# Sparse attention with a folded network: start-up loads in another order, value means copied by GpSimd, fewer engines with a written order

## The chip, the cores and the metric

The kernel runs on one core of one Trainium2 chip. The metric is device time in microseconds (us), from the start to the end of one execution; lower is better. The engines named below are TensorE (PE in the profile, with PEld for its weight loads), VectorE (DVE), ScalarE (ACT), GpSimd (POOL) and SyncE (SP), which here only issues transfers. One execution was also run under the hardware profiler; "the profile" and "the trace" are what it recorded.

## The reference

Attention over 4 batches, 8 heads, 768 positions, head size 64. Each position attends to the 31 positions around it and to 24 block summaries (the maximum of the keys of a block of 32, the mean of its values). The result is the input of a small network of four weight matrices, with no non-linearity but one product.

```python
k_sum = k.reshape(B, H, nb, block, D).max(axis=3)
v_sum = v.reshape(B, H, nb, block, D).mean(axis=3)
scores_l = scale * np.matmul(q, k.transpose(0, 1, 3, 2))     # kept where |i - j| < 16
scores_s = scale * np.einsum('bhsd,bhnd->bhsn', q, k_sum) + np.log(block)
a = softmax(concatenate([scores_l_m, scores_s], axis=-1))
x = np.matmul(a, concatenate([v, v_sum], axis=2))            # then 3072 tokens x 512
return ((x @ w1) * (x @ w2)) @ w3 @ w_out
```

## The kernel before

**Pairs and units.** Attention is done in 32 pairs: a pair is two heads (128 rows of head size) over half a batch (384 positions). Four pairs make a unit, whose four x tiles feed the network for 384 tokens. For one pair TensorE does the scores (`sc`, 6 matmuls, recorded in 12 halves), the transposes of the exponentials (`tp`) and the outputs (`po`); VectorE adds the mask and takes the minimum of the negated scores (L277), ScalarE does the exponentials (L291), and the results are split in a high and a low part for the float32r products (`keep_x`). The transposes of the first 8 pairs multiply by diagonals of the reciprocal sums; the later ones have the exponentials normalized by GpSimd (L300).

**Weights.** w3 and w_out are multiplied once (`fold_weights`: `wp[i]`, eight of 24 matmuls each), so that a unit costs the two products with w1 and w2 (`gate`: 16 accumulations of 12 matmuls, `mm<-x,w`) and one with `wp` (`project`). The weights come as 64-bit floats in 40 **pieces** of 128x512 (p0 to p39: eight of w_out, sixteen of w3, sixteen of w1 and w2). `piece` converts one: ScalarE L133, VectorE L139 and L140 (the 32-bit value), ScalarE L150 (its high part), VectorE L87 (its low part). Two pieces fill one tile `w`, and a matmul of `fold_weights` needs the piece that holds its columns. A piece's raw words lie in one of ten buffers (tag "ring"), which the rows of v for the means, batch 0's keys and later the `h` tiles share.

**The start.** A loop over steps t handles one piece a step, with the loads, the eight first pairs and the folding woven in: `FIRST` gives the step at which each of the first eight pairs begins, `LOADS` the extra transfers that follow a piece's, `WORK` the vector work of a step, `RATE` how much folding a step may emit. TensorE's stream takes from `stream` as many products as a step is due. Inside `manual_schedule(engines=...)` the engines named keep the order in which the code emits; the others are ordered by a scheduler from its own estimates. In this loop that is all five engines; in the loop behind it (pairs 8 to 31) only TensorE.

**The means of v.** For batch 0 the value means are a product: six matmuls (L219) of a constant matrix `mean_sb`, which is loaded, with rows of v. They come out at partitions 0 to 23, are copied to `vs0` (L537), and SyncE's transfers (L241, `load_sums`) carry them to the two partition ranges of each pair's value tile `v`, from 96 and from 32. Later batches take their means from `vB` on VectorE (L206, L207).

Of the kernel before, what the change touches and what calls it, by code (L numbers as in the profile page):

```python
# [11 lines left out]
F32 = mybir.dt.float32  # L12
# [14 lines left out]
PIECE = 512  # L27
AHEAD = 6

FIRST = (4, 8, 12, 16, 29, 34, 40, 43)  # L30
RING = 10


# [12 lines left out]
    return out  # L46


def mean_constants(n):

    rows = np.arange(n).reshape(-1, P).T
    return np.where(rows[:, :, None] // BLOCK == np.arange(n // BLOCK), 1.0 / BLOCK, 0.0).astype(np.float32)


@with_exitstack
def attention_moe(ctx, tc, qG, kW, kT, vP, vW, vB, mask, mean, w1, w2, w3T, wo, out):
    nc = tc.nc
    B, NPAIR, _, S = kT.shape
    NB = S // BLOCK
# [21 lines left out]
    halves = const.tile([P, 64], F32, name="halves")  # L81
    nc.gpsimd.tensor_tensor(halves, ident[:, :64], ident[:, 64:], ALU.add)
    mask_sb = const.tile([P, 3, COLS], F32, name="mask_sb")
    wp = [const.tile([P, 2, DO], F32R, name=f"wp{i}") for i in range(NF)]

    def low(eng, dst, src, hi):
# [21 lines left out]
        for at in range(0, n, PIECE):  # L108
            todo.append((src, shape, keep, at, min(n, at + PIECE)))

    begun = [0]
# [104 lines left out]
    def mean_products(tiles):  # L216
        po = ps.tile([P, 512], F32, name="means", tag="sc", bufs=4)
        for i in range(S // P):
            nc.tensor.matmul(  # L219
                po[:NB, :DM],  # L220
                lhsT=mean_sb[:, i],
                rhs=tiles[i // 2][:, i % 2],
                start=i == 0,
                stop=i == S // P - 1,
            )
        return po
# [118 lines left out]

    def keep_x(po, x):
        t = sb.tile([P, 2, U], F32R, name="x", bufs=7)
        full = sb.tile([P, U], F32, name="full")
        nc.scalar.copy(t[:, 0], po[:, :U])
        nc.vector.tensor_copy(full, po[:, :U])  # L350
        low(nc.vector, t[:, 1], full, t[:, 0])
        x.append(t)


# [2 lines left out]
    def gate(f, x, hs):  # L357
        acc = []
        for w in range(2):
            k = f * P // FQ  # L360
            while done[0] < NFOLD + PT * (2 * k + w + 1) or len(x) < NC:
                yield 0
            t = w12[w][k]
            fs = slice(f * P % FQ, f * P % FQ + P)
            a = ps.tile([P, 512], F32, name="mm", bufs=2)
            for c in range(NC):
                products(
                    a[:, :U],
                    [(t[:, 0, c, fs], x[c][:, 0]), (t[:, 1, c, fs], x[c][:, 0]), (t[:, 0, c, fs], x[c][:, 1])],
                    c == 0,  # L370
                    c == NC - 1,
                )
                yield 3 * U
            acc.append(a)
            if w == 0:
                g = sb.tile([P, U], F32, name="g")
                nc.scalar.copy(g, a[:, :U])  # L377
        nc.vector.tensor_tensor(g, acc[1][:, :U], g, ALU.mult)  # L378
        h = sb.tile([P, 2, U], F32R, name="h", tag="ring", bufs=RING)
        nc.vector.tensor_copy(h[:, 0], g)  # L380
# [110 lines left out]
    def first_pair(s):  # L491

        if s:
            prepare(s)
        u, sm, mx, sc = begin(s)
        yield
        fetch(s + 2)
# [5 lines left out]
        if s > 1:  # L503
# [18 lines left out]
    def later(work):  # L522
        delayed.append([2, work])

    kraws, vraws = {}, []

    def keys(p):
        kraws[p] = load_keys(0, p)

# [3 lines left out]
    def means():  # L533
        po = mean_products(vraws)
        vraws.clear()
        vs[0] = sb.tile([NB, DM], F32, name="vs0", tag="vs0", bufs=1)
        nc.scalar.copy(vs[0], po[:NB, :DM])  # L537

    mean_sb = aligned([P, S // P, NB], name="mean_sb", tag="sm", bufs=2)
    LOADS = {  # L540
        1: [lambda: keys(0), lambda: fetch(0)],
        3: [lambda: nc.sync.dma_start(mask_sb, mask)],
        4: [lambda: keys(1), lambda: fetch(1)],
        6: [lambda: nc.sync.dma_start(mean_sb, mean), lambda: rows(0)],
        7: [lambda: rows(1)],
        8: [lambda: rows(2)],
        10: [lambda: keys(2)],
        11: [lambda: fetch_values(0)],
        14: [lambda: fetch_values(1)],
        15: [lambda: keys(3)],  # L550
    }
    WORK = {
        2: [lambda: summaries(0, 0, kraws.pop(0)), lambda: fill(0)],
        6: [lambda: summaries(0, 1, kraws.pop(1))],
        8: [means],
        10: [lambda: fetch_sums(0), lambda: summaries(0, 2, kraws.pop(2))],
        12: [lambda: fetch_sums(1)],
        14: [lambda: summaries(0, 3, kraws.pop(3))],
    }
    RATE = 4600  # L560

    engines = mybir.EngineType
    with tc.manual_schedule(engines={engines.SP, engines.PE, engines.Activation, engines.DVE, engines.Pool}):
# [129 lines left out]
```

## Time and profile before

| what | value |
|---|---|
| median of 3 runs | 583.47 us (582.5 to 583.69) |
| the profiled execution's own time | 583.32 us |
| its span in the trace | 581.5 us |
| PE busy | 548.9 us, 94% of the span, 3948 matmuls |
| PEld busy | 486.1 us, 84% |
| DVE busy | 319.1 us, 55% |
| ACT busy | 220.2 us, 38% |
| POOL busy | 70.4 us, 12% |

Busy time is a share of the whole span, and the stages differ: the start is told from rows by time. A row of the timeline gives start, length, engine, line, what is written from what, and in brackets the idle time ahead of it with what ended it. A row of the chain of waits gives start, length and what the end of the program hung on at that time. A row of the groups gives busy time and the mean length of one in ns, then the idle time just ahead of the group's instructions and what ended it. Instructions of one engine overlap at their ends, so that in a dense stretch the distance from start to start is what one costs.

### The profile page before, as it was taken

What the parts mean: (1) busy time and instruction counts of PE and PEld (TensorE: products, weight loads), DVE (VectorE), ACT (ScalarE), POOL (GpSimd) and SP (SyncE); (2) the same over time, 40 slices, a digit from 0 to 9 for tenths busy, and PEclk for the clock granted to TensorE, in tenths of its full rate; (3) what the DMA queues carried; (4) which work ended last, traced back from release to release, by engine and by line L of the source; (5) the groups of instructions that cost most, each with busy time, mean ns of one, the idle gap of its engine ahead of it and who ended that gap; (6) DMA issues with size and microseconds to landing.
All of it is one profiled execution on the core that took longest, in us unless ns stands there. A gap on an engine that the chain in (4) does not pass through costs nothing.

```text
span 581.5 us, 10478 instructions
## 1 busy us (share of the span) xinstructions
PE 548.9 (94%) x3948; PEld 486.1 (84%) x3948; DVE 319.1 (55%) x872; ACT 220.2 (38%) x674; POOL 70.4 (12%) x96
## 2 busy tenths in 40 slices
PE   0768999999999999999999999999999999999997
PEld 0337787898789988998899989998999899988995
DVE  4857899797467532696246524662466246622330
ACT  4566776563533333333333233323332333331101
POOL 1000000000011211101111111111111111110000
PEclk9798999999999999999999999999999999999999
DMA  8998995523674122163221122112211222000001
GB/s 314 401 327 237 268 337 165 149 73 114 195 220 141 59 77 96 59 176 103 84 80 56 49 93 67 50 51 95 78 59 60 95 78 59 1 37 19 1 1 55
DMA packets 36290, 68.02 MB, mean 117 GB/s; under 512 B 4880, under 2 KB 19856, under 8 KB 36240
## 3 DMA queue, kind: packets, MB, share of 16 engines
q1 hardware_dynamic: 32784, 61.06, 33.1%
q10 hardware_dynamic: 3456, 6.29, 2.9%
q8 instruction: 31, 0.51, 0.4%
q14 instruction: 19, 0.16, 0.1%
HBM read 58.68 MB, written 6.29 MB: 112 GB/s over the span
## 4 chain that ended last, share of the span: by engine, by line
PE 86%; DVE 5%; DMA 4%; SPq 2%; ACT 1%; issue 1%; DVEq 0%; ACTq 0%
PE mm L91 72%; PE sc L263 5%; PE po L337 4%; PE tp L318 2%; PE tp L320 2%; DMA wraw<-in_wo_dram 1%; PE means L219 1%; DMA k<-in_kW_dram 1%; DMA v<-vs 1%; DMA raw<-in_vB_dram 1%; DVE sm L277 1%; ACT sm L291 1%; DVE ks L189 1%; DVE vs L206 1%; SPq L241 1%
## 5 line engine op out<-in xcount | busy, mean ns | idle before, releaser
L91 PE MATMUL mm<-x,w 128*128 128x384 f32 x1536 | 274.5, 336 | 2.6 <-DVE g L378 1.1
L91 PEld LDWEIGHTS mm<-x,w 128*128 128x128 f32 x1536 | 265.9, 188 | 7.1 <-DVE g L378 2.0
L91 PE MATMUL mm<-wp,h 128*128 128x512 f32 x576 | 137.2, 393 | 0.0
L91 PEld LDWEIGHTS mm<-wp,h 128*128 128x128 f32 x576 | 106.7, 188 | 22.5 <-issue 0.2
L377 ACT COPY g<-mm 128x384 f32<-128x384 f32 x64 | 30.6, 479 | 167.0 <-PE mm L91 167.0
L291 ACT ACTIVATE sm<-sm,mx 128x184 f32<-128x184 f32 x192 | 84.0, 440 | 17.6 <-DVE mx L277 17.5
L378 DVE TENSOR_TENSOR g<-mm,g 128x384 f32<-128x384 f32 x64 | 35.2, 551 | 88.9 <-PE mm L91 87.9
L326 DVE COPY pt<-tp 120x384 f32<-120x384 f32 x32 | 17.8, 556 | 87.0 <-PE tp L318 86.1
L277 DVE CUSTOM_DVE_ANT_0 sm<-sc,mask_sb 128x184 f32<-128x184 f32 x192 | 54.9, 345 | 5.9 <-PE sc L263 4.1
L296 POOL TENSOR_SCALAR mx<-mx 128x6 f32<-128x6 f32 x32 | 11.0, 345 | 387.9 <-ACT sm L291 355.5
L91 PE MATMUL mm<-w,w 128*128 128x512 f32 x192 | 49.6, 408 | 5.4 <-DVE w L87 5.3
L263 PE MATMUL sc<-k,q 64*128 64x184 f32 x384 | 39.5, 339 | 13.4 <-POOL k L252 13.4
L300 POOL TENSOR_TENSOR sm<-sm,mx 128x1104 f32<-128x1104 f32 x24 | 49.0, 2042 | 6.6 <-DVE mx L297 6.6
L91 PEld LDWEIGHTS mm<-w,w 128*128 128x128 f32 x192 | 35.8, 192 | 15.9 <-DVE w L87 6.6
L263 PEld LDWEIGHTS sc<-k,q 64*128 64x128 f32 x384 | 31.6, 196 | 15.4 <-POOL k L252 13.4
L325 ACT COPY pt<-tp 120x384 f32<-120x384 f32 x32 | 15.3, 478 | 65.3 <-PE tp L318 63.1
L380 DVE CAST h<-g 128x384 fp32r<-128x384 f32 x64 | 38.7, 605 | 2.0
L337 PEld LDWEIGHTS po<-pt,v 120*64 120x64 f32 x768 | 25.8, 140 | 14.3 <-issue 12.5
L87 DVE TENSOR_TENSOR h<-g,h 128x384 fp32r<-128x384 f32 x64 | 35.7, 558 | 2.0
L337 PE MATMUL po<-pt,v 120*64 120x64 f32 x768 | 30.3, 229 | 6.7 <-DMA v<-vs 6.1
L291 ACT ACTIVATION_READ_ACCUMULATOR sm<-sm,mx 128x1 f32 x192 | 36.2, 188 | 0.0
L397 ACT COPY wf<-mm 128x512 f32<-128x512 f32 x24 | 14.0, 581 | 53.7 <-PE mm L91 53.7
(32 smaller groups left out, 318.7 us busy)
## 6 DMA issues: line engine op xcount, KB each, us to landing
k<-in_kW_dram SPq DMA_DIRECT2D x32, 276.0 KB
wraw<-in_w3T_dram SPq DMA_DIRECT2D x16, 512.0 KB
wraw<-in_w_dram SPq DMA_DIRECT2D x16, 512.0 KB
raw<-in_kT_dram SPq DMA_DIRECT2D x16, 384.0 KB
q<-in_qG_dram SPq DMA_DIRECT2D x32, 192.0 KB
out_dram<-wf ACTq DMA_DIRECT2D x24, 256.0 KB
v<-in_vW_dram SPq DMA_DIRECT2D x32, 144.0 KB
raw<-in_vB_dram SPq DMA_DIRECT2D x12, 384.0 KB
```

The source lines that it names most:

```text
L87: eng.tensor_tensor(dst, src, hi.bitcast(F32), ALU.subtract)
L91: nc.tensor.matmul(acc, lhsT=a, rhs=b, start=first and i == 0, stop=last and i == len(terms) - 1)
L263: nc.tensor.matmul(sc[i // 2][h][:, i % 2 * COLS : (i % 2 + 1) * COLS], lhsT=q[rows, i * P : (i + 1) * P], rhs=k[rows, i], start=True, sto ...
L277: nc.vector.tensor_tensor_reduce(out=sm[:, j], in0=sc[i // 2][h][:, i % 2 * COLS : (i % 2 + 1) * COLS], in1=mask_sb[:, 0 if blk == 0 else ...
L291: nc.scalar.activation(sm[:, j], sm[:, j], AF.Exp, bias=mx[:, 0, j : j + 1], scale=-1.0, accum_out=mx[:, 1, j : j + 1])
L300: nc.gpsimd.tensor_tensor(sm, sm, mx[:, 2].unsqueeze(2).broadcast_to([P, NI, COLS]), ALU.mult)
L325: nc.scalar.copy(pt[0], tp[0][:KR, :U])
L326: nc.vector.tensor_copy(pt[1], tp[1][:KR, :U])
L337: nc.tensor.matmul(po[cols, at : at + 64], lhsT=v[:, g, i, cols], rhs=pt[g][:, (h * NBLK + i) * 64 : (h * NBLK + i + 1) * 64], start=True, ...
L377: nc.scalar.copy(g, a[:, :U])
L378: nc.vector.tensor_tensor(g, acc[1][:, :U], g, ALU.mult)
L380: nc.vector.tensor_copy(h[:, 0], g)
```

## The change

Six things change:

1. **The order of the first loads.** `LOADS` puts batch 0's keys, the mask, the rows of v and the later q, k and v tiles behind other pieces; `start_loads` issues an extra load only while the ring has room; q and k of pairs 2 and 3 and v of pairs 2 and 3 are loaded from this table. `FIRST` and `WORK` move to match.
2. **The value means of batch 0.** `mean_sb` is [128, 6, 128], set by GpSimd's memsets instead of a load, with the nonzero columns at 32 to 55 and 96 to 119. The product (now 120 rows instead of 24) so writes the means at both partition ranges, and GpSimd copies them into `v` instead of SyncE's transfers.
3. **No copy `full` in `keep_x`:** VectorE's low part reads the PSUM tile.
4. **The high part of `h` in `gate`** is cast by ScalarE instead of VectorE.
5. **Batch 1's blocks and keys** (the `coming` table) are loaded three and two pairs ahead instead of five to two.
6. **The start's `manual_schedule` names SP and PE only;** ScalarE, VectorE and GpSimd are ordered by the scheduler there too.

```diff
-FIRST = (4, 8, 12, 16, 29, 34, 40, 43)
+FIRST = (9, 13, 17, 21, 29, 33, 37, 41)
...
+    mean_sb = const.tile([P, S // P, P], F32, name="mean_sb")
+    nc.gpsimd.memset(mean_sb, 0.0)
+    for i in range(P // BLOCK):
+        for at in (CUT, CUT - 64):
+            part = mean_sb.rearrange("p t n -> p (t n)")[i * BLOCK : (i + 1) * BLOCK, at + i :: P + P // BLOCK]
+            nc.gpsimd.memset(part[:, : S // P], 1.0 / BLOCK)
...
-    def start_loads(n):
-        while todo and len(loading) < n:
+    def start_loads(at_least):
+        while todo or due_loads:
+            if len(loading) >= at_least and len(loading) + len(kraws) + len(vraws) + made[0] + 3 >= RING:
+                return
+            if due_loads:
+                due_loads.pop(0)()
+                continue
+            if len(loading) >= AHEAD:
+                return
...
-            for load_ in LOADS.pop(begun[0], ()):
-                load_()
+            due_loads.extend(LOADS.pop(begun[0], ()))
...
-                po[:NB, :DM],
-                lhsT=mean_sb[:, i],
+                po[:KR, :DM],
+                lhsT=mean_sb[:, i, :KR],
...
         for g, at in enumerate((CUT, CUT - 64)):
-            nc.sync.dma_start(v[at : at + NB, g], src.unsqueeze(1).broadcast_to([NB, NBLK, P]))
+            if b:
+                src = vs[b][p * NB : (p + 1) * NB]
+                nc.sync.dma_start(v[at : at + NB, g], src.unsqueeze(1).broadcast_to([NB, NBLK, P]))
+            else:
+                src = vs[b][at : at + NB, p * P : (p + 1) * P]
+                nc.gpsimd.tensor_copy(v[at : at + NB, g], src.unsqueeze(1).broadcast_to([NB, NBLK, P]))
...
-        full = sb.tile([P, U], F32, name="full")
         nc.scalar.copy(t[:, 0], po[:, :U])
-        nc.vector.tensor_copy(full, po[:, :U])
-        low(nc.vector, t[:, 1], full, t[:, 0])
+        low(nc.vector, t[:, 1], po[:, :U], t[:, 0])
...
-        nc.vector.tensor_copy(h[:, 0], g)
+        nc.scalar.copy(h[:, 0], g)
...
-        for at, step in zip((5, 5, 4, 4, 3, 3, 2, 2), steps):
+        for at, step in zip((3, 3, 3, 3, 2, 2, 2, 2) if b == 1 else (5, 5, 4, 4, 3, 3, 2, 2), steps):
...
-        8: [means],
-        10: [lambda: fetch_sums(0), lambda: summaries(0, 2, kraws.pop(2))],
+        12: [lambda: summaries(0, 1, kraws.pop(1)), means],
+        14: [lambda: fetch_sums(0)],
...
-    with tc.manual_schedule(engines={engines.SP, engines.PE, engines.Activation, engines.DVE, engines.Pool}):
-        start_loads(AHEAD)
+    with tc.manual_schedule(engines={engines.SP, engines.PE}):
+        start_loads(0)
```

Where it moves instructions is seen in the built programs. The first place is SyncE's queue at the very start; `wraw<-in_wo_dram` and `wraw<-in_w3T_dram` are pieces of w_out and w3, `raw` the keys for the summaries. Before:

```order
L117 DMA wraw<-in_wo_dram 128x1024 x2
L184 DMA raw<-in_kT_dram 128x768
L247 DMA q<-in_qG_dram 128x384
L248 DMA k<-in_kW_dram 128x552
L117 DMA wraw<-in_w3T_dram 128x1024 x2
L542 DMA mask_sb<-in_mask_dram 128x552
L117 DMA wraw<-in_wo_dram 128x1024
```

And SyncE's queue of the changed program from its start, up to the rows of v for the means:

```order
L128 DMA wraw<-in_wo_dram 128x1024 x2
L128 DMA wraw<-in_w3T_dram 128x1024 x2
L128 DMA wraw<-in_wo_dram 128x1024 x3
L194 DMA raw<-in_kT_dram 128x768
L261 DMA q<-in_qG_dram 128x384
L262 DMA k<-in_kW_dram 128x552
L128 DMA wraw<-in_wo_dram 128x1024 x2
L552 DMA mask_sb<-in_mask_dram 128x552
L128 DMA wraw<-in_wo_dram 128x1024
L128 DMA wraw<-in_w3T_dram 128x1024
L223 DMA rows<-in_vP_dram 128x2x512 x2
```

Seven pieces now stand ahead of pair 0's keys instead of two. Behind these rows follow a piece, the third of the three loads of `rows`, and the keys, q and k of pair 1.

The second place is TensorE's queue from its start. `mm<-w,w` is folding (24 matmuls for one `wp`), `means` the product with `mean_sb`. Before:

```order
L263 MATMUL sc<-k,q 128x184 x6
L91 MATMUL mm<-w_120,w_145 128x512 x6
L91 MATMUL mm<-w_178,w_145 128x512 x6
L219 MATMUL means<-rows,mean_sb 24x512 x6
L263 MATMUL sc<-k,q 128x184 x6
L91 MATMUL mm<-w_223,w_145 128x512 x6
L320 MATMUL tp<-diag,sm 120x64 x12
L91 MATMUL mm<-w_286,w_145 128x512 x6
L337 MATMUL po<-pt,v 64x64 x12
```

The same queue of the changed program, from its start to pair 0's transposes:

```order
L93 MATMUL mm<-w_115,w_137 128x512 x6
L93 MATMUL mm<-w_157,w_137 128x512 x6
L93 MATMUL mm<-w_183,w_137 128x512 x6
L277 MATMUL sc<-k,q 128x184 x6
L93 MATMUL mm<-w_211,w_137 128x512 x6
L229 MATMUL means<-rows,mean_sb 120x512 x6
L93 MATMUL mm<-w_115,w_257 128x512 x6
L93 MATMUL mm<-w_157,w_257 128x512 x3
L277 MATMUL sc<-k,q 128x184 x6
L93 MATMUL mm<-w_157,w_257 128x512 x3
L93 MATMUL mm<-w_183,w_257 128x512 x6
L334 MATMUL tp<-diag,sm 120x64 x12
```

The first 24 folding matmuls now all stand ahead of the means, and 24 more stand between the means and what follows; behind these rows come 18 folding matmuls and then pair 0's `po`.

The third place is where the value means reach `v`. Before, in SyncE's queue, between pieces of w3 (`v<-vs_263` are the means, `k` and `q` those of pair 3):

```order
L184 DMA raw<-in_kT_dram 128x768
L247 DMA q<-in_qG_dram 128x384
L248 DMA k<-in_kW_dram 128x552
L117 DMA wraw<-in_w3T_dram 128x1024
L241 DMA v<-vs_263 24x3x128 x2
L117 DMA wraw<-in_w3T_dram 128x1024 x2
```

In the changed program they stand in GpSimd's queue, ahead of the sums of pair 1's exponentials (`mx`):

```order
L266 COPY k<-ks 128x3x24
L310 TENSOR_SCALAR mx<-mx 128x6
L266 COPY k<-ks 128x3x24
L255 COPY v<-vs_301 24x384 x4
L310 TENSOR_SCALAR mx<-mx 128x6
L266 COPY k<-ks 128x3x24
L255 COPY v<-vs_301 24x384 x4
```

Sixteen such copies, two for each of the eight pairs of batch 0, take the place of sixteen transfers.

More of the change, by code (lines that the diff above doesn't have):

```diff
@@ L46, in mask_constants, with attention_moe @@
     return out
-def mean_constants(n):
-    rows = np.arange(n).reshape(-1, P).T
-    return np.where(rows[:, :, None] // BLOCK == np.arange(n // BLOCK), 1.0 / BLOCK, 0.0).astype(np.float32)
 @with_exitstack
-def attention_moe(ctx, tc, qG, kW, kT, vP, vW, vB, mask, mean, w1, w2, w3T, wo, out):
+def attention_moe(ctx, tc, qG, kW, kT, vP, vW, vB, mask, w1, w2, w3T, wo, out):
     nc = tc.nc
@@ L109, in weight @@
             todo.append((src, shape, keep, at, min(n, at + PIECE)))
-    begun = [0]
-    def start_loads(n):
-        while todo and len(loading) < n:
+    begun, due_loads, kraws, vraws = [0], [], {}, []
+    def start_loads(at_least):
[7 more added lines that the diff above has]
+                return
             src, shape, keep, at, to = todo.pop(0)
@@ L496, in first_pair @@
         yield
-        fetch(s + 2)
+        if s + 2 >= NPAIR:
+            fetch(s + 2)
         reduce(u, 0, sc, sm, mx)
@@ L502, in first_pair @@
         yield
-        if s > 1:
+        if s >= NPAIR:
             fetch_values(s)
@@ L523, in later @@
         delayed.append([2, work])
-    kraws, vraws = {}, []
     def keys(p):
@@ L535, in means @@
         vraws.clear()
-        vs[0] = sb.tile([NB, DM], F32, name="vs0", tag="vs0", bufs=1)
-        nc.scalar.copy(vs[0], po[:NB, :DM])
-    mean_sb = aligned([P, S // P, NB], name="mean_sb", tag="sm", bufs=2)
+        vs[0] = sb.tile([KR, DM], F32, name="vs0", tag="vs0", bufs=1)
+        nc.scalar.copy(vs[0], po[:KR, :DM])
     LOADS = {
[L541 to L550, printed above, removed]
+        6: [lambda: keys(0), lambda: fetch(0)],
+        8: [lambda: nc.sync.dma_start(mask_sb, mask)],
+        10: [lambda: rows(0), lambda: rows(1)],
+        11: [lambda: rows(2), lambda: keys(1), lambda: fetch(1)],
+        13: [lambda: fetch_values(0)],
+        14: [lambda: keys(2), lambda: fetch(2)],
+        16: [lambda: fetch_values(1)],
+        18: [lambda: keys(3), lambda: fetch(3)],
+        20: [lambda: fetch_values(2)],
+        22: [lambda: fetch_values(3)],
     }
     WORK = {
-        2: [lambda: summaries(0, 0, kraws.pop(0)), lambda: fill(0)],
-        6: [lambda: summaries(0, 1, kraws.pop(1))],
-        8: [means],
-        10: [lambda: fetch_sums(0), lambda: summaries(0, 2, kraws.pop(2))],
-        12: [lambda: fetch_sums(1)],
-        14: [lambda: summaries(0, 3, kraws.pop(3))],
+        8: [lambda: summaries(0, 0, kraws.pop(0)), lambda: fill(0)],
+        12: [lambda: summaries(0, 1, kraws.pop(1)), means],
+        14: [lambda: fetch_sums(0)],
+        16: [lambda: summaries(0, 2, kraws.pop(2)), lambda: fetch_sums(1)],
+        20: [lambda: summaries(0, 3, kraws.pop(3))],
+        21: [lambda: fetch_sums(2)],
+        23: [lambda: fetch_sums(3)],
     }
@@ L568, in attention_moe @@
         while next_piece or old or pairs or delayed or t <= FIRST[-1]:
-            start_loads(max(1, min(AHEAD, RING - 3 - made[0])))
+            start_loads(1)
             now, next_piece = next_piece, None
@@ L666 @@
     mask = mask_constants(NB, scale)
-    mean = mean_constants(S)
     def words(w, n):
@@ L680 @@
     for name, a in (
-        ("qG", qG), ("kW", kW), ("kT", kT), ("vP", vP), ("vW", vW), ("vB", vB), ("mask", mask), ("mean", mean),
+        ("qG", qG), ("kW", kW), ("kT", kT), ("vP", vP), ("vW", vW), ("vB", vB), ("mask", mask),
         ("w1", tiles(moe_w1)), ("w2", tiles(moe_w2)), ("w3T", w3T), ("wo", wo),
```

1 line of the change is left out of this document (removed).

## The prediction

> **What bounds the kernel now.** The page first: how busy is TensorE, and when is it not? The second row is its busy share in 40 slices of 14.5 us.
>
> ```profile
> span 581.5 us, 10478 instructions
> PE   0768999999999999999999999999999999999997
> ```
>
> From the fifth slice on TensorE is full; only the first four hold waits. So the time is TensorE's work plus what it waits at the start, and nothing off TensorE counts unless TensorE waits for it. The timeline of TensorE shows the waits one by one (in brackets, with what ended them):
>
> ```profile
> 13.41 2.21 PE L263 MATMUL sc<-k,q 64*128 64x184 f32 x12 [13.41 <-POOL k L252]
> ...
> 20.55 0.96 PE L91 MATMUL mm<-w,w 128*128 128x512 f32 x3 [1.36 <-DVE w L87]
> 23.88 0.80 PE L91 MATMUL mm<-w,w 128*128 128x512 f32 x1 [2.37 <-DVE w L87]
> 24.61 7.11 PE L219 MATMUL means<-rows,mean_sb 128*24 128x512 f32 x12
> ...
> 38.87 0.50 PE L91 MATMUL mm<-w,w 128*128 128x512 f32 x1 [1.56 <-DVE w L87]
> 45.51 1.55 PE L337 MATMUL po<-pt,v 120*64 120x64 f32 x24 [6.14 <-DMA v<-vs]
> ```
>
> The groups show all that TensorE waited after that: 2.6 for the gates, 0.8 for a transpose, and in the `po` group 0.6 besides the 6.1 above, 4.0 us in all.
>
> ```profile
> L91 PE MATMUL mm<-x,w 128*128 128x384 f32 x1536 | 274.5, 336 | 2.6 <-DVE g L378 1.1 <-ACT g L377 0.6 <-DVE w L87 0.6
> L320 PE MATMUL tp<-diag,sm 64*120 64x64 f32 x192 | 12.2, 269 | 0.8 <-DVE full L350 0.8
> L337 PE MATMUL po<-pt,v 120*64 120x64 f32 x768 | 30.3, 229 | 6.7 <-DMA v<-vs 6.1 <-ACT pt L325 0.6
> ```
>
> The chain of waits gives the price of each kind of work where TensorE is dense, and the slow stretch after its long wait:
>
> ```profile
> 39.69 5.68 DMA v<-vs
> ...
> 45.51 1.55 PE po L337 x24
> 47.06 1.97 PE sc L263 x12
> ...
> 60.12 1.14 PE sc L263 x12
> ...
> 63.53 1.41 PE tp L320 x24
> 64.93 4.31 PE mm L91 x18
> 69.24 0.85 PE po L337 x24
> ...
> 577.96 0.58 ACT wf L397
> ```
>
> A folding matmul costs 4.31 / 18 = 0.239 us, the scores of a pair 1.14, its transposes 1.41, its outputs 0.85. TensorE ends at 577.96; the last copy and store take 3.54 more of the span.
>
> The wait of 6.14 is the largest that can go. The means were ready long before:
>
> ```profile
> 31.76 0.57 ACT L537 COPY vs<-means 24x512 f32<-24x512 f32 x1 [4.44 <-PE means L219]
> ```
>
> They were copied by 32.3, but SyncE issued their transfer at 39.69, after the loads queued ahead of it, and it landed at 45.4. And a wait costs twice: the windows show the granted clock (the first figure behind POOL's) fall.
>
> ```profile
> 21.50:22.50 1.00, 0.01 (x1) 0.00 (x0) 1.00 (x3) 1.00 (x4) 0.02 (x1) 0.50 1.06 414
> ...
> 43.00:45.50 2.50, 0.00 (x0) 0.02 (x1) 0.00 (x0) 0.00 (x0) 0.00 (x0) 0.50 0.98 316
> ```
>
> Half the clock makes `po` 1.55 instead of 0.85 and the next `sc` 1.97 instead of 1.14: 1.5 us behind the long wait.
>
> **The change, part by part: up to the means.** TensorE's matmuls are the same in number and in columns moved. The sum goes by one milestone, the end of the means (24.61 + 7.11 = 31.72 before).
>
> Loads first. Piece 0 (512 KB, from 128x1024 words) was taken up at 4.90, piece 7, before which 6660 KB had been asked for, at 21.37:
>
> ```profile
> 4.90 0.66 ACT L133 ACTIVATE wf<-wraw 128x512 f32<-128x512 f32 x1 [2.90 <-DMA wraw<-in_wo_dram]
> ...
> 21.37 0.66 ACT L133 ACTIVATE wf<-wraw 128x512 f32<-128x512 f32 x1 [1.64 <-DMA wraw<-in_wo_dram]
> ```
>
> That is (6660 - 512) / 16.47 = 373 KB a us. In the new order the third load of rows ends at 8808 KB, so at 27.1, pair 1's k at 9660 KB, 29.4, and pair 0's v at 10972 KB, 33.0. Seven pieces in a row arrive every 1.4 us, and VectorE takes longer for each, as rows of a dense stretch show:
>
> ```profile
> 94.63 0.68 DVE L87 TENSOR_TENSOR w<-wf,w 128x512 fp32r<-128x512 f32 x1
> 95.23 0.41 DVE L139 TENSOR_SCALAR wf<-wf 128x512 uint32<-128x512 uint32 x1
> 95.68 0.69 DVE L140 SCALAR_TENSOR_TENSOR wf<-wraw,wf 128x512 uint32<-128x512 uint32 x1
> 96.29 0.69 DVE L87 TENSOR_TENSOR wp<-mm,wp 128x512 fp32r<-128x512 f32 x1
> 96.89 0.34 DVE L277 CUSTOM_DVE_ANT_0 sm<-sc,mask_sb 128x184 f32<-128x184 f32 x1
> ...
> 97.16 0.34 DVE L277 CUSTOM_DVE_ANT_0 sm<-sc,mask_sb 128x184 f32<-128x184 f32 x1
> ```
>
> From start to start a piece is 0.60 + 0.45 + 0.61 = 1.66, a store of `wp` 0.60, a reduction 0.27. So VectorE, not the loads, paces the new start. It begins with piece 0:
>
> ```profile
> 5.59 0.43 DVE L139 TENSOR_SCALAR wf<-wf 128x512 uint32<-128x512 uint32 x1 [5.59 <-ACT wf L133]
> ```
>
> Ahead of the means stand all 24 matmuls of the first fold, which need pieces 0 to 9: ten pieces 16.6, one key summary 0.95 (group row below), three reductions 0.8, and about 0.8 of waits for ScalarE's parts: 24.8, the last three matmuls 0.7, so the means start at 25.5. Their fifth matmul needs the third load of rows at 27.1, when four of 0.86 or more have run (28.9): covered by 1.8. They took 7.11 before, partly at half clock; the dense end below gives 0.43 a record, 5.1 for twelve.
>
> ```profile
> 29.41 2.31 PE L219 MATMUL means<-rows,mean_sb 128*24 128x512 f32 x5
> ```
>
> Bounds: 25.5 + 5.1 = 30.6, and 25.5 + 7.1 with 1.1 more if the scores too run at half clock, 33.7. I take **32.0**, the middle. The load of `mean_sb` goes; GpSimd's nine memsets, at some 0.24 each by its shortest copy below, lie in its idle time long before 25.5.
>
> The Trainium skill has a rule here (TensorE: Matmul & The Clock Gate, "Why this matters for your kernels"): no TensorE gaps over about 3 us, or the clock halves. The new start has no gap over 2 us after its first matmul, so by it the means would run at full clock, and the sum below would be 1.4 lower. The rows above disagree: the clock was already 0.50 at 21.5 after waits of 1.36 and less.
>
> **After the means.** Before, from 31.72 to 577.96 are 546.2 us. Off go the waits 1.56 + 6.14 + 4.0 and the slow 1.5: 533.0 of dense work. The order of TensorE has 12 more folding matmuls done ahead of the means, 2.9 less: **530.1**. What does TensorE wait now?
>
> - The sums of v: ScalarE copies the means at 32.0 + 0.6, GpSimd copies them to `v`. `po` stands behind 36 folding matmuls, the scores of pair 1 and a transpose: 8.6 + 1.1 + 1.4 = 11.2 after the means, 43.2; pair 0's v is there at 33.0. The price of a copy of 24x384 isn't in the trace; nearest are a 128x72 copy, 0.24, and the two-input 128x1104, 2.03, which by elements would be 0.71:
>
> ```profile
> 22.48 0.24 POOL L252 COPY k<-ks 128x72 f32<-128x72 f32 x1 [9.13 <-DVE ks L189]
> ...
> 305.31 2.03 POOL L300 TENSOR_TENSOR sm<-sm,mx 128x1104 f32<-128x1104 f32 x1 [0.31 <-DVE mx L297]
> 305.69 1.86 DVE L380 CAST h<-g 128x384 fp32r<-128x384 f32 x1
> ...
> 308.82 0.36 DVE L380 CAST h<-g 128x384 fp32r<-128x384 f32 x1
> ```
>
>   Four copies are at most 2.8 us: the 6.14 and its 1.5 go, with some 7 us of cover.
> - VectorE's order has piece 11's low part behind two reductions of pair 1's scores: TensorE waits about **0.5**.
> - VectorE is full from there to the last fold. By the order of the built program it does, from pair 1's first reduction to the last store of `wp`, 21 pieces, 24 reductions, 7 stores, 8 evacuations and 2 key summaries:
>
> ```profile
> L326 DVE COPY pt<-tp 120x384 f32<-120x384 f32 x32 | 17.8, 556 | 87.0 <-PE tp L318 86.1 <-PE tp L320 0.5
> L189 DVE TENSOR_REDUCE ks<-raw 128x24 f32<-128x768 f32 x16 | 15.0, 946 | 1.8 <-DMA raw<-in_kT_dram 1.8
> ```
>
>   34.9 + 6.5 + 4.2 + 4.5 + 1.9 = 52.0, from 3.1 after the means (nine folding matmuls 2.2, then the scores' first tile 0.9): done 55.1 after the means; the last fold's own end puts its store at 55.9. TensorE needs that store, to reuse the accumulator, when 168 folding matmuls, four pairs' `sc`, `tp`, `po` and one accumulation of 2.3 are done: 40.2 + 13.6 + 0.5 + 2.3 = 56.6. Slack 0.7. The rows above also show GpSimd stopping VectorE: the cast took 1.86 beside GpSimd's 2.03, and 0.36 alone. Ten of the copies fall in this stretch, between 0 and 7 us of VectorE. I take 2 (they get in between some operations, beside others that read PSUM nothing): **1.4** of wait, bounds 0 and 6.4.
> - Of the later 4.0, between none and all stay: **2.1**, the middle, since `full` (32 of 0.56) and the casts (64) leave VectorE but the gates still wait for g; the casts on ScalarE, some 0.5 us each by its copies, come between TensorE's needs (with that cover gone, the slower rival below). GpSimd's and VectorE's new order from the scheduler I cost at nothing beyond these: the weights' low parts lie several us ahead of TensorE.
>
> Sum: 32.0 + 530.1 + 0.5 + 1.4 + 2.1 = 566.1, the tail 3.54 makes a span of 569.6, and 1.8 outside the span (583.32 - 581.5) **571.5 us**, against 583.32 of the same execution, which is 0.15 below the median of the runs. The 11.8 gained are the 6.14, 1.5 and 1.56, the 2.9 of folding done sooner, less 0.3.
>
> **The rivals.**
>
> *VectorE becomes the bound at the first gates.* For: it was busy 17.45 of 18 us there before, and the slack is 0.7.
>
> ```profile
> 80.00:98.00 18.00, 18.00 (x106) 14.69 (x106) 17.45 (x36) 10.88 (x23) 0.00 (x0) 1.00 0.61 211
> ```
>
>   Each of ten copies stopping VectorE for its whole 0.71, and a later gate caught too: 5 to 7 more, 577 to 579. Against: most copies lie where VectorE is ahead of TensorE. The Trainium skill has this as a rule (SBUF — State Buffer, "SBUF: two separate sides"): GpSimd and a two-input VectorE operation take a shared port in turn, whole instruction by whole instruction. The cast's 1.86 agrees; by the rule alone the time is the 577 to 579 above. Chance 0.13.
>
> *The full clock holds from the first fold on,* and the wait at the gates is nothing: 1.4 + 1.4 + 1 less, 567. Chance 0.06.
>
> *Slower.* ScalarE is strictly in order; the cast of `h` now waits in it for VectorE's g, and ahead of the next g copy that frees an accumulator. If that copy comes late at one gate of each of the 24 later pairs by 0.7, that is 17 us: 588. It turns slower from 0.5 a pair (11.8 / 24). Against: the copy is due 2.3 us after the cast's input, and ScalarE sat idle before it:
>
> ```profile
> 306.08 0.48 ACT L377 COPY g<-mm 128x384 f32<-128x384 f32 x1 [1.48 <-PE mm L91]
> ```
>
>   Chance 0.08.
>
> *The change doesn't do what it says:* the scheduler's order puts the copies or pair 0's evacuation so late that `po` waits as before: 583. The order shown speaks against it. Chance 0.03.
>
> **How the numbers follow.** The forecast, 571.5, has 0.70; its own bounds are 30.6 with waits of 1.5 (567.6) and 33.7 with the gates' 6.4 (578.2). The range, 567 to 579, takes in the first two rivals and leaves the slower one and most of the third out. A measurement can tell 0.2%, about 1.2 us. Faster: 0.70 + 0.13 + 0.06, 0.89; within: 0.03; slower: 0.08.
>
> **What would show it.** Right: no `DMA v<-vs` ahead of the first `po`; the means end near 32; `po` of pair 0 near 43 at full clock; a wait of 0 to 3 us for `wp` or g near 86 to 90. Wrong: TensorE waiting for low parts between 33 and 86, means ending after 34, or g copies named ahead of gates in every later pair.

## The result and the profile after

The changed kernel takes 568.16 us in the median of 4 runs (567.94 to 569.15), the kernel before beside it 583.4: 15.2 us faster, a ratio of 0.9745 with a 95% interval of 0.9728 to 0.9761. Predicted were 571.5 and a range of 567 to 579. The profiled execution took 569.15 us, its span is 567.4. The page of the changed kernel first, again its span and TensorE's busy share in 40 slices:

```profile
span 567.4 us, 10460 instructions
PE   2899999999999999999999999999999999999997
```

Two slices at the start are now short of 9, where four were. TensorE's timeline at the start (start, length, what, count, and in brackets the idle time ahead with what ended it):

```profile
10.90 0.79 PE L93 MATMUL mm<-w,w 128*128 128x512 f32 x1 [10.90 <-ACT w L160]
12.05 4.00 PE L93 MATMUL mm<-w,w 128*128 128x512 f32 x8 [0.35 <-DVE w L89]
16.51 1.65 PE L93 MATMUL mm<-w,w 128*128 128x512 f32 x3 [0.46 <-ACT w L160]
19.03 1.65 PE L93 MATMUL mm<-w,w 128*128 128x512 f32 x3 [0.88 <-ACT w L160]
21.01 1.65 PE L93 MATMUL mm<-w,w 128*128 128x512 f32 x3 [0.33 <-ACT w L160]
22.59 2.16 PE L277 MATMUL sc<-k,q 64*128 64x184 f32 x12
...
25.84 0.97 PE L93 MATMUL mm<-w,w 128*128 128x512 f32 x3 [0.43 <-DVE w L89]
26.98 0.50 PE L93 MATMUL mm<-w,w 128*128 128x512 f32 x1 [0.17 <-DVE w L89]
27.32 5.31 PE L229 MATMUL means<-rows,mean_sb 128*120 128x512 f32 x12
...
37.19 1.44 PE L93 MATMUL mm<-w,w 128*128 128x512 f32 x5 [0.20 <-DVE w L89]
...
44.27 0.92 PE L351 MATMUL po<-pt,v 120*64 120x64 f32 x24
...
87.39 8.51 PE L93 MATMUL mm<-x,w 128*128 128x384 f32 x48
```

The first `po`, at 44.27, has no bracket: the wait of 6.14 for the sums of v is gone. The gates' 48 matmuls at 87.39 have none either. What carries the sums now stands in ScalarE's and GpSimd's timelines:

```profile
32.67 0.59 ACT L548 COPY vs<-means 120x512 f32<-120x512 f32 x1 [0.55 <-PE means L229]
```
```profile
33.39 2.17 POOL L255 COPY v<-vs 24x384 f32<-24x384 f32 x4 [0.69 <-ACT vs L548]
```

The four copies of the first two pairs are done at 35.6, 8.7 us ahead of the first `po`. From there on little is waited for; the groups of TensorE and the two rows that hold what is left:

```profile
L93 PE MATMUL mm<-x,w 128*128 128x384 f32 x1536 | 273.7, 336 | 1.2 <-DVE g L390 1.2
L351 PE MATMUL po<-pt,v 120*64 120x64 f32 x768 | 29.6, 226 | 0.7 <-ACT pt L339 0.7
```

With the 0.20 at 37.19 that is 2.2 us behind the means. The chain of waits ends with TensorE at 563.90:

```profile
512.62 51.26 PE mm L93 x270
563.90 0.58 ACT wf L409
```

Where the 14.1 us of span came from shows in three points of TensorE's timeline, which serve for the experiments too: the start of the first gate matmul (`mm<-x,w`), of the first matmul with `wp`, and the end of the span. Read from each kernel's trace, in us; the median and the ratio are of all its runs:

| kernel | first gate | first `wp` | span | median | ratio, 95% interval |
|---|---|---|---|---|---|
| before | 98.03 | 142.58 | 581.5 | 583.4 | |
| after | 87.39 | 131.75 | 567.4 | 568.16 | 0.9745 [0.9728, 0.9761] |
| e1 sums by SyncE | 97.39 | 142.52 | 576.7 | 576.43 | 0.9894 [0.9876, 0.9911] |
| e2 written order | 86.81 | 146.31 | 582.7 | 584.48 | 1.0029 [1.0016, 1.0041] |
| e3 cast on VectorE | 87.58 | 131.97 | 566.5 | 568.12 | 0.9744 [0.9730, 0.9757] |
| e4 copies alone | 90.04 | 134.61 | 572.4 | 574.38 | 0.9853 [0.9838, 0.9868] |
| e6 copies, free order | 88.59 | 132.92 | 570.3 | 572.36 | 0.9813 [0.9792, 0.9834] |
| e7 copies twice | 87.64 | 132.58 | 567.1 | 569.19 | 0.9762 [0.9745, 0.9779] |
| e8 means first | 87.36 | 132.00 | 569.9 | 569.83 | 0.9760 [0.9739, 0.9782] |
| e9 written order, early blocks | 86.95 | 138.41 | 574.2 | 574.97 | 0.9861 [0.9841, 0.9881] |
| e10 early blocks | 88.00 | 133.22 | 568.5 | 570.19 | 0.9770 [0.9748, 0.9793] |
| e11 VectorE ordered | 92.64 | 148.56 | 584.5 | 586.84 | 1.0062 [1.0045, 1.0078] |
| e13 VectorE's shift twice | 90.57 | 135.77 | 571.6 | 573.72 | 0.9846 [0.9823, 0.9868] |
| e14 ScalarE and GpSimd ordered | 88.10 | 137.13 | 572.9 | 574.18 | 0.9839 [0.9820, 0.9857] |

Of the 14.1, 10.6 were won by the first gate, 0.2 from there to `wp`, 3.3 behind it. Up to the first gate both orders hold the same work. The last two figures are not for equal work: between the first gate and the first `wp` the changed order has the scores and transposes of three pairs where the old one has two, by the prices of the prediction 1.14 + 1.41 = 2.55 us more. At equal work 2.7 were won there, where the kernel before waited 2.2 and the changed one nothing, and 0.7 behind it. e4 and e6 have the old order of TensorE, all the others the new one.

The kernel before, run beside each of these, had medians of 583.17 to 583.76, so a difference of two medians in the table is good to about half a us.

### The profile page after: what moved, and what is told of

The parts are those of the page before. It is cut to its first block, busy times and chain, and to the rows that moved or that the text cites. A ratio compares the mean times of both kernels' runs of the same rounds, so it can differ in the third digit from the quotient of the medians.

```text
span 567.4 us, 10460 instructions
## 1 busy us (share of the span) xinstructions
PE 548.2 (97%) x3948; PEld 485.8 (86%) x3948; DVE 279.5 (49%) x776; ACT 253.6 (45%) x738; POOL 79.0 (14%) x121
## 4 chain that ended last, share of the span: by engine, by line
PE 93%; DVE 3%; DMA 2%; ACT 1%; issue 0%; SPq 0%; DVEq 0%; ACTq 0%
PE mm L93 78%; PE sc L277 5%; PE po L351 5%; PE tp L334 2%; PE tp L332 2%; DMA wraw<-in_w3T_dram 1%; PE means L229 1%; DMA raw<-in_kT_dram 1%; DVE w L89 1%; DVE wf L150 1%; DVE vs L216 0%; ACT w L160 0%; DVE ks L199 0%; DVE wf L149 0%; DVE g L390 0%
## 5 line engine op out<-in xcount | busy, mean ns | idle before, releaser
L392 ACT CAST h<-g 128x384 fp32r<-128x384 f32 x64 | 32.8, 513 | 111.1 <-DVE g L390 111.1
L93 PE MATMUL mm<-w,w 128*128 128x512 f32 x192 | 54.5, 430 | 13.7 <-ACT w L160 12.6
L89 DVE TENSOR_TENSOR h<-g,h 128x384 fp32r<-128x384 f32 x64 | 53.4, 834 | 27.0 <-ACT h L392 26.9
L310 POOL TENSOR_SCALAR mx<-mx 128x6 f32<-128x6 f32 x32 | 7.7, 241 | 379.3 <-ACT sm L305 370.7
L339 ACT COPY pt<-tp 120x384 f32<-120x384 f32 x32 | 15.2, 475 | 49.6 <-PE tp L332 43.2
```

The lines of the kernel that those rows point to most:

```text
L89: eng.tensor_tensor(dst, src, hi.bitcast(F32), ALU.subtract)
L93: nc.tensor.matmul(acc, lhsT=a, rhs=b, start=first and i == 0, stop=last and i == len(terms) - 1)
L339: nc.scalar.copy(pt[0], tp[0][:KR, :U])
L392: nc.scalar.copy(h[:, 0], g)
```

## The experiments

**The copies, taken out of the new kernel and put alone into the old one.**

```diff
-                nc.gpsimd.tensor_copy(v[at : at + NB, g], src.unsqueeze(1).broadcast_to([NB, NBLK, P]))
+                nc.sync.dma_start(v[at : at + NB, g], src.unsqueeze(1).broadcast_to([NB, NBLK, P]))
```

> The changed kernel with one part undone: the sums of v go to the value tiles by SyncE's transfers again, at the place in the order where GpSimd's copies stood. Theory A (the copies carry the gain): SyncE stands at the transfer until the means are copied at 33.3, the loads behind it come late, and the transfer itself needs 5.7 us and more, so that po of pair 0 at 44.3 or pair 1's a little later waits; the time goes up by 4 to 8 us, 572 to 576. Theory B (it was only SyncE's queue, and the new order of the loads cures that by itself): SyncE issues at 33.3, it lands near 40, 4 us ahead of po, and VectorE, not the loads, sets the pace behind it: at most 1 us more, 568 to 569.

Theory A: 576.43, 8.3 us more than the changed kernel. SyncE's queue and TensorE's timeline of this kernel:

```profile
42.28 0.33 SPq L128 DMA_DIRECT2D wraw<-in_w3T_dram  x1
42.70 2.16 SPq L255 DMA_DIRECT2D v<-vs  x2
```
```profile
51.90 1.65 PE L351 MATMUL po<-pt,v 120*64 120x64 f32 x24 [7.31 <-DMA v<-vs]
53.48 3.98 PE L93 MATMUL mm<-w,w 128*128 128x512 f32 x9
```

The expectation had one thing wrong: SyncE didn't stand at the transfer for the means. It reached it 9 us after they were copied, since it was late with the loads ahead; then it took 9.2 us until `po` could start. The new order of the loads doesn't cure the old wait: with it the wait is 1.2 longer. The clock falls behind the wait as it did before: nine folding matmuls take 3.98 here and 2.33 in the rows of a dense stretch.

The same part alone in the kernel before (with `mean_sb` made by the memsets, the product 120 rows high, and no tile `full`, for which there is no room beside it):

```diff
-        src = vs[b][p * NB : (p + 1) * NB] if b else vs[b][:, p * P : (p + 1) * P]
+                nc.gpsimd.tensor_copy(v[at : at + NB, g], src.unsqueeze(1).broadcast_to([NB, NBLK, P]))
...
-        full = sb.tile([P, U], F32, name="full")
-        nc.vector.tensor_copy(full, po[:, :U])
```

> The kernel before with the means written by their product where GpSimd copies them from, mean_sb made by memsets, and without the tile full (there is no room for it beside the larger mean_sb); its order of loads, its order of engines and its casts stay. Theory A (the prediction's term): the wait of 6.14 for v and the slow clock of 1.5 behind it go, and nothing takes their place: 583.4 - 7.6 = 575.8, 575 to 577. Theory B: the wait gives way to another in the same place (the load of v's own tile, queued in SyncE, or the evacuation of the transposes), and 2 us or less are won: 581 to 583.

574.38, 9.0 us won of the 15.2, 1.4 more than the 7.6 of the prediction's term. Of these, 8.0 are there at the first gate; the 1.1 behind the first `wp` may belong to `full`, which this kernel leaves out too. Its TensorE:

```profile
38.55 0.50 PE L97 MATMUL mm<-w,w 128*128 128x512 f32 x1 [1.77 <-DVE w L93]
38.99 0.92 PE L347 MATMUL po<-pt,v 120*64 120x64 f32 x24
```

No wait for v, full clock behind it, and nothing in its place: theory A. The waits of the gates behind (2.6 before, 2.4 here) and for a transpose (0.8 before, 0.3 here) hardly changed.

**The written order in the new kernel.**

```diff
-    with tc.manual_schedule(engines={engines.SP, engines.PE}):
+    with tc.manual_schedule(engines={engines.SP, engines.PE, engines.Activation, engines.DVE, engines.Pool}):
```

> The changed kernel with all five engines kept in the written order in the start, as before. The prediction costed the scheduler's order of ScalarE, VectorE and GpSimd at nothing: by it 567.5 to 569. Rival: the freed order is worth something of its own, since VectorE paces the start and a key summary or a reduction that stands ahead of a weight's low part makes TensorE wait at each such place: 2 to 5 us more, 570 to 573, with waits for w or g on TensorE between 33 and 90.

584.48: with the order alone undone the whole gain is gone. Neither expectation fits, the first in its size, the rival in its place, for the table shows the start as good as the changed kernel's up to the first gate (86.81 against 87.39); all of it is lost between there and the first `wp`, 59.5 us for 44.4. TensorE, VectorE and SyncE of this kernel:

```profile
115.98 2.38 PE L93 MATMUL mm<-x,w 128*128 128x384 f32 x12
125.23 2.29 PE L93 MATMUL mm<-x,w 128*128 128x384 f32 x6 [6.88 <-DVE g L390]
127.45 2.67 PE L334 MATMUL tp<-diag,sm 64*120 64x64 f32 x24
130.05 5.17 PE L93 MATMUL mm<-x,w 128*128 128x384 f32 x15
```
```profile
115.12 1.17 DVE L216 TENSOR_REDUCE vs<-raw 96x32 f32<-96x1024 f32 x1
...
116.42 1.21 DVE L216 TENSOR_REDUCE vs<-raw 96x32 f32<-96x1024 f32 x1
...
119.50 1.22 DVE L216 TENSOR_REDUCE vs<-raw 96x32 f32<-96x1024 f32 x1 [1.67 <-DMA raw<-in_vB_dram]
...
122.69 1.22 DVE L216 TENSOR_REDUCE vs<-raw 96x32 f32<-96x1024 f32 x1 [1.75 <-DMA raw<-in_vB_dram]
...
124.03 0.68 DVE L89 TENSOR_TENSOR w<-wf,w 128x512 fp32r<-128x512 f32 x1
124.63 0.55 DVE L390 TENSOR_TENSOR g<-mm,g 128x384 f32<-128x384 f32 x1
```
```profile
88.13 29.84 SPq L209 DMA_DIRECT2D raw<-in_vB_dram  x4
```

VectorE stands at the reductions of batch 1's value blocks, waiting for their transfers, and a gate's `g` stands behind them. The wait of 6.88 and the clock behind it (0.50 in the mean from 125.2 to 135.0, so some 4.9 us) make 11.8 of the 15.1 lost in this stretch. The last two transfers are late because of VectorE's order itself: the tile `raw` of the later batches has two buffers (L189), and SyncE issued the third block at 116.3 and the fourth at 117.7, as the first and the second reduction ended (115.12 + 1.17, 116.42 + 1.21). Of its 29.84 us over the four issues it waited 19.6 for VectorE ahead of the third alone, by the waits of its queue. In the changed kernel the same row is half as long: the four reductions lie at 100.9, 103.1, 105.8 and 108.1, between other work of VectorE, with no wait ahead of them, and the third and fourth issue again follow the ends of the first two, at 102.1 and 104.3:

```profile
88.52 16.09 SPq L209 DMA_DIRECT2D raw<-in_vB_dram  x4
```

So the question is whether this is the one place, and whose order it is. First the lead of these loads put back, in the written order:

```diff
-        for at, step in zip((3, 3, 3, 3, 2, 2, 2, 2) if b == 1 else (5, 5, 4, 4, 3, 3, 2, 2), steps):
+        for at, step in zip((5, 5, 4, 4, 3, 3, 2, 2), steps):
```

> All five engines in the written order, as in e2_written_order, and the lead of batch 1's blocks back at 5, 5, 4, 4 pairs where the change has 3, 3, 3, 3. Theory A (e2's loss is one place: in the written order VectorE stands at four reductions of vs whose loads were asked for late, from 115.1 to 124.0, ahead of a low part of w and a gate's g; TensorE waited 6.88 there and then ran at half clock): with two of the four a pair earlier and their loads two pairs earlier that wait goes with its slow clock, some 6.9 + 5 us: 570 to 573. Theory B (the written order costs at many places in the start): 580 or more stays.

574.97: 9.5 us come back, somewhat less than theory A's least, and the wait of 6.88 is gone. Between first gate and `wp` it still takes 51.5 against 44.4, in small waits (1.12 and 0.72 for `g`, 1.04 for `pt` are the largest) and a clock of 0.76 from 125 to 132. One place held more than half, not all. The same lead with the freed order:

> The changed kernel with only the lead of batch 1's blocks back at 5, 5, 4, 4 pairs. Theory A (the freed order puts the reductions where TensorE isn't kept waiting, wherever their loads stand): 567.5 to 569. Theory B (the later loads of the blocks are themselves part of the gain, since earlier ones take VectorE's time and SyncE's queue ahead of the first gates, where VectorE is full): 2 us or more, 570 to 573, with waits between 60 and 100 on TensorE.

570.19, with runs from 568.77 to 570.63: the interval overlaps that of the changed kernel, so whether the later blocks are worth up to 2 us or nothing stays open. Theory B's waits between 60 and 100 did not come: there is one, of 0.59 for `wp`. Set against e9, freeing the order is worth 4.8 us with the old lead, and 16.3 with the new one.

Then one engine at a time, with the new lead:

```diff
-    with tc.manual_schedule(engines={engines.SP, engines.PE}):
+    with tc.manual_schedule(engines={engines.SP, engines.PE, engines.DVE}):
```

> The changed kernel with VectorE's order kept as written beside TensorE's and SyncE's, ScalarE's and GpSimd's left to the scheduler. It tells whose freed order the 16 us of e2_written_order were. Theory A (VectorE's: it stands at the four reductions of vs from 115 to 124 ahead of a gate's g): 580 to 585, with the wait of about 7 for g near 125. Theory B (ScalarE's, which stood 3.1, 2.7, 7.9 and 5.0 us at casts of h waiting for VectorE's g): 570 or less.

586.84, above theory A's range, and not by its mechanism alone. The four reductions stand together as in e2, from 120.8 to 128.4, two of them behind waits for their transfers, but no wait of 7 for `g` follows: TensorE waits 1.28 for `g`, 2.10 for `w` and 1.39 without a cause in the trace, and its clock is 0.76 from 130 to 138. In all 11.6 us are lost between the first gate and `wp`. And 5.3 are lost ahead of the first gate, where e2 lost nothing. A written VectorE beside a free GpSimd and ScalarE has a wait that is in neither of the others:

```profile
38.34 2.07 PE L277 MATMUL sc<-k,q 64*128 64x184 f32 x12 [2.79 <-POOL k L266]
```

And the counterpart:

```diff
-    with tc.manual_schedule(engines={engines.SP, engines.PE}):
+    with tc.manual_schedule(engines={engines.SP, engines.PE, engines.Activation, engines.Pool}):
```

> The counterpart: ScalarE's and GpSimd's order kept as written beside TensorE's and SyncE's, VectorE's left to the scheduler. Theory A: 567.5 to 570. Theory B: 576 to 585. If both this one and the one before stay above 575, the two orders are needed together.

574.18, between the theories: 6.0 us more. The gates' group has 4.0 of waits instead of 1.2; these 2.8 are about half of the 6.0:

```profile
L93 PE MATMUL mm<-x,w 128*128 128x384 f32 x1536 | 275.1, 336 | 4.0 <-DVE g L390 2.1 <-ACT g L389 1.9
```

Both orders cost, VectorE's most; and they don't add up: 18.7 and 6.0 apart, 16.3 together in e2.

**The freed order without the new loads:** e4's kernel with only SP and PE named.

> The kernel of e4_copies_alone (574.4) with only TensorE's and SyncE's order kept in the start, so the old order of the loads with the freed order. Theory A (the freed order only mends what the later blocks would cost, as e2 suggests; with the old lead it has little to mend): 573.5 to 575. Theory B (the freed order by itself brings what lies between 574.4 and 568.2): 567.5 to 570.

572.36, between the two: 2.0 us beyond e4. So the copies (with `full` gone) bring 9.0, the freed order 2.0 with the old loads, and the rest, 4.2, is the new loads, the casts and the later blocks together; no run has the new loads alone.

**The cast of `h`.**

```diff
-        nc.scalar.copy(h[:, 0], g)
+        nc.vector.tensor_copy(h[:, 0], g)
```

> The changed kernel with the high part of h written on VectorE again. The trace of the changed kernel has waits for g of 1.25 us in all after the first gates, where the kernel before had 1.1 + 0.6. Theory A: VectorE is ahead of TensorE at the gates in either form, and the cast costs no more than the 0.4 us that it takes once on VectorE, at a gate or two: 568 to 569.5. Theory B: the hold of GpSimd on VectorE strikes the cast and the low part one after the other (0.61 + 0.56 before against 0.83 now), so that the waits at the gates come back and more of them: 2 us or more, 570 to 572.

568.12 against 568.16: the cast's engine is worth nothing, theory A. VectorE's group shows why the move saves it less than the cast's time. After the change the low part takes the hold that the cast had beside GpSimd's long multiplication, 834 ns in the mean for 558 before:

```profile
L89 DVE TENSOR_TENSOR h<-g,h 128x384 fp32r<-128x384 f32 x64 | 53.4, 834 | 27.0 <-ACT h L392 26.9
```

**What sets the start.** The means first on TensorE, with their loads after pieces 2 and 3:

```diff
+        2: [lambda: rows(0), lambda: rows(1)],
+        3: [lambda: rows(2)],
...
+        4: [means],
...
-        12: [lambda: summaries(0, 1, kraws.pop(1)), means],
+        12: [lambda: summaries(0, 1, kraws.pop(1))],
```

> The changed kernel with the three loads of rows asked for after pieces 2 and 3, and the means' matmuls on TensorE at step 4, ahead of the first key summary's and the scores'. It tells what sets the start. Theory A (VectorE, busy 18.95, 19.16 and 17.48 us of 20, 20 and 18 from 40 to 98 in the changed kernel, is the limit up to the first gates; the means need nothing of it): TensorE gets ahead by up to 5 and gives most of it back in waits for w and g before 95, so 566 to 568.5. Theory B (TensorE's own work is the limit): 4 us or more are won, 562 to 564. Rival C: the pieces come 5.8 us later (2148 KB at 373 KB a us) and VectorE starves for them: 570 to 574.

569.83, slower if anything, and by neither A nor C as told. Its TensorE:

```profile
9.54 7.34 PE L229 MATMUL means<-rows,mean_sb 128*120 128x512 f32 x12 [9.54 <-DMA rows<-in_vP_dram]
...
44.24 0.92 PE L351 MATMUL po<-pt,v 120*64 120x64 f32 x24
...
247.88 8.09 PE L93 MATMUL mm<-x,w 128*128 128x384 f32 x36 [1.92 <-DVE g L390]
```

The means are done 16 us sooner, yet the first `po` starts at 44.24 for 44.27 and the first gate at 87.36 for 87.39: the pieces come later, as rival C said, and cost just what the means gave. Nothing is lost there either. The profiled execution, the longest of the five, shows a loss far behind: VectorE stands 1.99 us ahead of a key reduction for its transfer; TensorE waits 1.92 for the `g` behind it and then runs slower (36 gate matmuls take 8.09 for 6.51 in the changed kernel). The changed kernel has a wait at the same place, of 1.25, without the slow stretch. Why the other four runs, too, are above the changed kernel's median is open.

VectorE's share, measured with its shortest operation on a piece done twice:

```diff
-        nc.vector.tensor_scalar(out=bits, in0=c, scalar1=3, scalar2=None, op0=ALU.logical_shift_left)
+        for _ in range(2):
+            nc.vector.tensor_scalar(out=bits, in0=c, scalar1=3, scalar2=None, op0=ALU.logical_shift_left)
```

> The changed kernel with the shift of every weight piece (the operation of 0.42 on VectorE, 40 of them) done twice. Theory A (VectorE sets the pace from the first piece to the gates): ten more of 0.34 to 0.45 ahead of the means, less the 3 us that VectorE sat idle from 5 to 25, then 21 more up to the first gates with some 5 us idle: 4 to 8 us late at the gates, 572 to 576. Theory B (TensorE's own work and the loads set it): 570 or less.

573.72, 5.6 us more: theory A, though less of it is seen at the gates than was said: the means start 2.8 later (30.14 for 27.32), the first gate 3.2, the first `wp` 4.0. The windows of the changed kernel (behind the stretch its length, then busy time of PE, PEld, DVE, ACT and POOL, the clock, the transfers' share and GB/s) show how little room there was:

```profile
40.00:60.00 20.00, 20.00 (x153) 15.61 (x153) 18.95 (x44) 16.90 (x47) 5.47 (x10) 1.00 1.02 320
60.00:80.00 20.00, 20.00 (x160) 15.91 (x157) 19.16 (x46) 16.78 (x43) 0.80 (x3) 1.00 0.87 329
80.00:98.00 18.00, 18.00 (x120) 15.99 (x117) 17.48 (x45) 16.16 (x42) 1.72 (x4) 1.00 0.65 175
```

and of this kernel, where VectorE has none left:

```profile
40.00:60.00 20.00, 20.00 (x168) 15.70 (x167) 19.93 (x57) 16.84 (x49) 3.46 (x7) 1.00 1.01 331
60.00:80.00 20.00, 19.49 (x145) 15.42 (x145) 20.00 (x52) 17.34 (x48) 3.56 (x7) 1.00 0.83 286
```

**What the copies cost VectorE:** each done twice.

```diff
-                nc.gpsimd.tensor_copy(v[at : at + NB, g], src.unsqueeze(1).broadcast_to([NB, NBLK, P]))
+                for _ in range(2):
+                    nc.gpsimd.tensor_copy(v[at : at + NB, g], src.unsqueeze(1).broadcast_to([NB, NBLK, P]))
```

> The changed kernel with every one of GpSimd's copies of the value sums done twice (32 for 16, 12 of the new ones between 33 and 90). It measures what the copies cost VectorE, which the prediction put at 2 us for ten, 1.4 of it as a wait at the first gates. Theory A (each holds VectorE for most of its 0.56): 12 x 0.56 = 6.7 less some 2 us of room, 3 to 5 more, 571 to 573. Prediction's own share (0.2 a copy): 2.4 less the room, 568 to 569.5. Theory B (they get in between VectorE's operations): 567.5 to 568.8, and no wait at the gates.

569.19, 1.0 more, with overlapping intervals. The first gate moves by 0.25, with no wait there. Theory A falls. The time lies in the range of the prediction's own share and a little above theory B's, while the missing wait is theory B's sign: the two can't be told apart. By the sums of these rows against those above, from 40 to 98, GpSimd is busy 7 us longer (15.05 for 7.99), and VectorE needs 56.02 us for 133 instructions where it had 55.59 for 135, 1.3 us more for the same number, an estimate, as the instructions are not quite the same:

```profile
40.00:60.00 20.00, 20.00 (x155) 15.50 (x153) 19.31 (x44) 17.13 (x49) 9.59 (x15) 1.00 1.03 337
60.00:80.00 20.00, 20.00 (x151) 15.91 (x153) 19.47 (x47) 16.81 (x43) 2.02 (x5) 1.00 0.83 305
80.00:98.00 18.00, 18.00 (x124) 15.99 (x123) 17.24 (x42) 15.81 (x41) 3.44 (x6) 1.00 0.66 169
```

No kernel tried is faster than the changed one beyond what a measurement can tell; e3's 568.12 is the same.

## Why the prediction was right

The median, 568.16, is 3.3 below the forecast. About 1.0 of it is that the profiled execution, at 569.15, was the longest of the four. The rest is in the sum: it gave 569.6 of span, and 567.4 came. The three terms, the means, the dense work and the waits, are off by +0.6, -1.0 and -1.8.

- **The means, 32.0.** They ended at 32.63 (27.32 + 5.31), within the bounds, by two errors that nearly cancel. They started 1.8 later than the 25.5 reckoned from VectorE's rows, which allowed it 0.8 of waits: it lost 1.95 waiting for ScalarE's results and 1.14 for the first scores, of which these two rows are the longest. And they ran at full clock, 5.31 instead of the 6.5 in between. That VectorE paces the start was right, and e13 shows it.

```profile
20.99 0.69 DVE L89 TENSOR_TENSOR w<-wf,w 128x512 fp32r<-128x512 f32 x1 [0.68 <-ACT w L160]
...
24.22 0.35 DVE L291 CUSTOM_DVE_ANT_0 sm<-sc,mask_sb 128x184 f32<-128x184 f32 x1 [1.14 <-PE sc L277]
```

- **Dense work, 530.1.** From 32.63 to TensorE's end at 563.90 are 531.3; less the 2.2 of waits 529.1. Where the 1.0 went is open.
- **The sums of v.** Reckoned at 6.14 + 1.5 gone. Right, shown from both sides: 8.3 lost by e1, 9.0 won by e4, 8.0 of these by the first gate. The four copies took 2.17, 0.54 each, where 0.24 to 0.71 was reckoned, with 8.7 us of cover where 7 was said.
- **The loads, 2.9 + 1.56 - 0.3 = 4.2.** What e6 leaves to the changed kernel is 4.2 too, but that holds the casts and the later blocks as well, and only 1.2 of it is there at the first gate (88.59 against 87.39). No run shows that the agreement is more than chance.
- **The wait at the first gates, 1.4.** It was nothing. VectorE's last store of `wp` was reckoned at 55.9 after the means and 2 more for the copies, 57.9, and TensorE's need at 56.6. The store ended 56.6 after them, by the row below, and the need was at 87.39 + 2.27 (twelve gate matmuls), 57.0 after them. So the mis-sized term is VectorE's time up to there, 1.3 too long. The hold of the copies was, by the estimate above, not far off: in e7 9 more instructions of GpSimd between 40 and 98 (the counts of the windows) cost VectorE about 1.3, 0.14 each for the 0.2 taken. The room left is 0.4.

```profile
88.55 0.69 DVE L89 TENSOR_TENSOR wp<-mm,wp 128x512 fp32r<-128x512 f32 x1
```

- **Later waits, 2.1, and piece 11's 0.5.** 2.0 and 0.2. But the 2.1 was the middle of an unknown, and its reason, fewer operations on VectorE, is not what decides: e3 puts 64 casts back and waits less, 0.6 in its trace.
- **"GpSimd's and VectorE's new order from the scheduler I cost at nothing."** This is the step that failed, though the sum doesn't show it. The place it was judged by, the low parts from 33 to 86, was right: e2 has the same start. It isn't where the order works. The change also asks for batch 1's blocks later, and a written order would have held VectorE for them between the first gates and `wp`: 16.3 us with the new lead, 4.8 with the old. The prediction gave the later blocks no term and took the stretch behind the first gates as dense. That no loss came there is luck as far as the prediction goes: an edit that it valued at zero took it away.
- **The rivals.** VectorE as the bound, 577 to 579: it is close to the bound (e13), but not through the copies. By the Trainium skill (SBUF — State Buffer, "SBUF: two separate sides"), GpSimd and a two-input operation of VectorE take a port in turn by whole instructions; the low part of `h`, up to 2.42 us beside GpSimd's 2.03, agrees; the copies show it weakly, 7 us more of GpSimd cost VectorE 1.3. The cast that the prediction gave as its example reads one input, not two. Full clock from the first fold, 567: half so; three matmuls took 1.65 up to 22.7 and 0.97 from 25.84 on, and the means were quick. The slower rival, ScalarE's cast late for the next `g`, is what e14 has in small: with ScalarE's order written its gates wait 1.9 for ScalarE's `g` at three places in the start; free, none there and none in the 24 later pairs.

Had the parts been judged by undoing one at a time, they would have seemed worth 8.3 (copies), 16.3 (freed order), 0 (cast) and some 2 (later blocks), far more than 15.2 together: the loads, the lead of the blocks and the freed order hang on each other.

## What to carry to other kernels

A transfer that waits in a queue behind loads can be late by the queue however its data stand; a copy by an idle engine that needs no queue takes the wait away, and here that held with either order of loads. When loads are moved later, look for the engine that consumes them in a fixed order, for what stands behind that instruction, and for how many buffers hold the loads: it is there, not at the load, that the cost appears, and a free order on that engine may hide it. An edit that only frees an order can be worth mostly what the other edits would break (here 2.0 by itself, 16.3 with them), so it is priced with them.

## What the runs showed that was not expected

- **SyncE stood 29.84 us over four issues** in e2 and 16.09 in the changed kernel, at the same four loads. In both the third and the fourth follow the end of a reduction that frees one of the two buffers; a third buffer was not tried.
- **Short waits and the clock.** A wait of 1.92 in e8 was followed by a granted clock of 0.80 in the mean from 250 to 256; one of 1.25 at the same place in the changed kernel by none. The rule that the prediction weighed (the Trainium skill, TensorE: Matmul & The Clock Gate, "Why this matters for your kernels": no gap over about 3 us) does not cover e8's. The row gives the stretch, its length, the busy time of TensorE, the clock, the transfers' share and GB/s:

```profile
250.00:256.00 6.00, 6.00 (x29) 0.80 0.03 10
```

- **A slow stretch that the clock's record does not show.** Until 22.7 us three folding matmuls of the changed kernel take 1.65, and eight 4.00, 0.50 us each, where a dense stretch at a clock of 1.00 has 0.26 (nine in 2.33). The record stands at 1.00 from the start all the same:

```profile
15.00:20.00 5.00, 3.66 (x8) 1.00 1.03 412
20.00:25.00 5.00, 4.67 (x18) 1.00 1.03 394
```
